# Moving an early sum ahead of the values of the last two key heads, splitting a projection into column groups and moving the denominators in a decode kernel

## Chip, cores, metric

One core of one Trainium2 chip. The metric is the device time of one execution in microseconds; each number given for a kernel is the median of its runs. The kernel before took 190.9 us (three runs, 190.2 to 194.06; the slowest was in a slower state that some executions fall into, over 1.5% above the fastest). TensorE does the matmuls, VectorE and ScalarE the element-wise work. The granted clock is the share of its full speed at which TensorE was allowed to run. The experiments ran in four sessions, each on another chip, so across sessions times are compared by their ratios to the kernel before, which ran beside each.

## The reference

One token for each of two sequences: layer norm, attention over the last 4096 positions of a key and value cache (16 query heads, 8 key heads, head size 256), a dense Mish layer, both added to the input.

```python
xn = _layernorm(x)
q  = (xn @ wq)                       # 2 x 16 heads x 256
k  = k_cache[:, :, Sk - W:, :]       # W = 4096, 8 heads, each for 2 query heads
v  = v_cache[:, :, Sk - W:, :]
p  = softmax(q k^T * 256 ** -0.5)
out = x + (p v).reshape(B, 1, 4096) @ wo + mish(xn @ w1 + b1) @ w2
```

Nearly all of the 77.8 MB that it reads are keys and values, 4 MB of each for every key head.

## The kernel before

The loop goes over the key heads `i`. In turn `i` the keys of head `i` are scored in four pieces (VectorE transposes, TensorE scores, ScalarE exponentials, VectorE transposes p into `pT`), and the values of head `i - 1` are summed. Heads 0 to 5 use `values` (32 matmuls 512 columns wide). Heads 6 and 7 use `values_fixed`: 128 matmuls of only four columns, each with its own weight load of 128 x 128 values. The projection of each head by `wo` adds to one sum, `psE` (2 x 448, `add`). Head 7 alone goes to `psA`, the same sum laid out as four column groups of 112 at partitions 0, 32, 64 and 96 (`add_last`); `carry` copies `psE` into it first.

```python
    def add_last(lhsT, w, start=False, stop=False):
        for n in range(NO):                               # NO = 4 column groups
            nc.tensor.matmul(part(n), lhsT=lhsT, rhs=w[:, n * DO : (n + 1) * DO],
                             start=start, stop=stop, tile_position=(0, n * Q), ...)

    def carry():
        early = consts.tile([Bsz, D], FP32, name="early")
        nc.vector.tensor_copy(out=early[:], in_=psE[:])
        add_last(ident_f[0:Bsz, 0:Bsz], early[:, :], start=True)
    # ... cut ...
    def values_fixed(i):
        state["rec", i] = denominator(i)                  # f32 matmul with ones, reciprocal
        # ... cut: po, vv ...
        for t in range(T):                                # T = 64
            for c in range(ND):                           # ND = 2
                nc.tensor.matmul(po[:, c, :], lhsT=vv[:, t, c, :], rhs=pTv[:, th, 0:Q:HS], ...)
        scale_o(i, po)                                    # oT = po * rec, on VectorE
    # ... cut: loop over i up to Hkv = 8 ...
        else:                                             # i == 8
            mix(i - 2)                                    # head 6: add() into psE
            carry()
        # ... cut ...
        if i == Hkv:
            mix(i - 1)                                    # head 7: add_last() into psA
```

The softmax here doesn't subtract the row's maximum and nothing guards it: scores larger than these inputs give would overflow.

## Time and profile before

| | kernel before |
|---|---|
| time, median of its 3 runs | 190.9 us |
| span in the profile | 189.2 us |
| TensorE instructions of which the trace has records (weight loads and matmuls) | 2154 |
| values of head 6 end | 178.54 us |
| values of head 7 begin | 182.22 us |
| last projection ends | 186.54 us |

The last three rows are read from the chain of what ended last, in order of time, where a line ends at its start plus its length. The prediction below shows that chain.

### The profile page before, as it was taken

How to read it: one execution, taken by the hardware profiler on the slowest of the kernel's cores; microseconds unless marked ns; L12 is line 12 of the kernel's file. 1: busy time of each engine (PE TensorE's matmuls, PEld its weight loads, DVE VectorE, ACT ScalarE, POOL GpSimd, SP SyncE). 2: the span in 40 equal slices, each digit the busy share in tenths (PEclk: the TensorE clock that was granted, in tenths of full speed). 3: DMA queues.
4: the chain of work that ended last, by engine and by line, in shares of the span. 5: the costliest groups of instructions: out<-in, count | busy, mean ns of one | idle time of the engine just before them, and what ended most of it. 6: DMA issues, size and time to landing. Idle time of an engine off the chain costs nothing.

```text
span 189.2 us, 2687 instructions
## 1 busy us (share of the span) xinstructions
PE 152.6 (81%) x1077; PEld 76.2 (40%) x1077; DVE 108.1 (57%) x144; ACT 45.4 (24%) x148; POOL 16.4 (9%) x74
## 2 busy tenths in 40 slices
PE   0396088905989997978995899999996969999983
PEld 0132033901434453425442463436442624464762
DVE  6504497059570995099603983299307986955311
ACT  3004015200242233024222204224312242233201
POOL 7000600300003001200030000300020000000000
PEclk9999669955999999999999657999999999999755
DMA  6999899999999999998999999999999999999970
GB/s 208 429 466 443 380 451 422 430 440 443 416 443 443 436 435 438 436 436 360 489 416 411 436 443 436 440 423 424 456 419 443 419 409 443 430 430 416 414 300 0
DMA packets 4597, 77.82 MB, mean 411 GB/s; under 512 B 485, under 2 KB 1001, under 8 KB 1898
## 3 DMA queue, kind: packets, MB, share of 16 engines
q1 hardware_dynamic: 4580, 77.66, 96.2%
q8 instruction: 8, 0.13, 0.2%
q14 instruction: 3, 0.02, 0.0%
q10 hardware_dynamic: 6, 0.01, 0.0%
HBM read 77.67 MB, written 0.00 MB: 411 GB/s over the span
## 4 chain that ended last, share of the span: by engine, by line
DMA 57%; PE 21%; DVE 19%; ACT 1%; issue 1%; SPq 0%; ACTq 0%; DVEq 0%
DMA k<-in_A_k_cache_dram 57%; DVE kt L414 14%; PE sc L426 8%; PE o L487 4%; PE q L573 4%; PE q L527 3%; DVE pT L452 3%; PE psE L223 2%; PE psA L240 1%; ACT p L440 1%; SPq L112 0%; PE den L468 0%; DVE early L252 0%; DVE osum L548 0%; DVE oTm L556 0%
## 5 line engine op out<-in xcount | busy, mean ns | idle before, releaser
L414 DVE STREAM_TRANSPOSE kt<-k 128x2048 f32<-128x2048 f32 x32 | 73.1, 2288 | 49.4 <-DMA k<-in_A_k_cache_dram 49.4
L426 PE MATMUL sc<-kt,qdiag 128*128 128x512 bf16 x256 | 64.2, 400 | 17.6 <-DVE kt L414 16.9
L440 ACT ACTIVATE p<-sc,off 128x256 bf16<-128x256 f32 x64 | 33.0, 544 | 71.3 <-PE sc L426 70.6
L426 PEld LDWEIGHTS <-qdiag 128*128 128x128 bf16 x256 | 23.8, 99 | 54.1 <-issue 22.5
L487 PE MATMUL o<-v,pT 128*8 128x512 bf16 x192 | 42.5, 379 | 0.0
L487 PEld LDWEIGHTS <-pT 128*8 128x8 bf16 x192 | 17.2, 92 | 22.4
L452 DVE STREAM_TRANSPOSE pT<-p 128x512 bf16<-128x512 bf16 x32 | 21.8, 682 | 6.6 <-ACT p L440 6.5
L292 POOL COPY qdiag<-qt 32x16 bf16<-32x16 bf16 x64 | 12.9, 247 | 121.5 <-PE sc L426 104.7
L496 ACT COPY o_sb<-o 8x512 f32<-8x512 f32 x12 | 6.3, 573 | 36.3 <-PE o L487 36.3
L527 PEld LDWEIGHTS q<-ident_f,o_sb 8*64 8x64 f32 x192 | 13.2, 147 | 3.0 <-issue 3.0
L527 PE MATMUL q<-ident_f,o_sb 8*64 8x4 f32 x192 | 13.7, 203 | 0.0
L440 ACT ACTIVATION_READ_ACCUMULATOR p<-sc,off 128x1 f32 x64 | 11.7, 183 | 0.0
L272 PE MATMUL q_ps<-v,xq 128*128 128x512 bf16 x28 | 8.5, 479 | 3.0 <-DMA v<-in_A_wq_dram 3.0
L223 PE MATMUL psE<-v,act_bf 128*2 128x448 bf16 x14 | 4.2, 471 | 6.6 <-DVE act_bf L360 6.6
L573 PEld LDWEIGHTS <-v 128*128 128x128 bf16 x256 | 7.3, 102 | 0.0
L573 PE MATMUL q<-pT,v 128*128 128x4 bf16 x256 | 7.1, 168 | 0.0
L272 PEld LDWEIGHTS <-xq 128*128 128x128 bf16 x28 | 3.3, 118 | 8.2 <-issue 3.9
L282 DVE CAST q_sb<-q_ps 128x512 bf16<-128x512 f32 x2 | 1.3, 686 | 8.9 <-PE q_ps L272 8.9
L223 PE MATMUL psE<-wo,oTm 128*2 128x448 bf16 x24 | 5.0, 352 | 0.8 <-DVE oTm L556 0.8
L223 PEld LDWEIGHTS <-act_bf 128*2 128x2 bf16 x14 | 1.4, 105 | 9.0 <-DVE act_bf L360 6.7
L282 ACT CAST q_sb<-q_ps 128x512 bf16<-128x512 f32 x2 | 1.1, 589 | 13.5 <-PE q_ps L272 13.5
L193 PE MATMUL xnT_ps<-ident,xn_bf 2*128 2x2 bf16 x7 | 0.5, 166 | 4.6 <-DVE xn_bf L136 4.6
(62 smaller groups left out, 46.6 us busy)
## 6 DMA issues: line engine op xcount, KB each, us to landing
k<-in_A_k_cache_dram SPq DMA_DIRECT2D x7, 4096.0 KB, 29.1
v<-in_A_v_cache_dram SPq DMA_DIRECT2D x7, 4096.0 KB, 27.0
k<-in_A_k_cache_dram SPq DMA_DIRECT2D x2, 2048.0 KB, 26.3
v<-in_B_w_dram SPq DMA_DIRECT2D x2, 1568.0 KB, 24.9
wo<-in_A_wo_dram SPq DMA_DIRECT2D x3, 896.0 KB, 31.0
v<-in_A_wq_dram SPq DMA_DIRECT2D x1, 2048.0 KB, 7.8
v<-in_A_v_cache_dram SPq DMA_DIRECT2D x1, 2048.0 KB, 14.1
v<-in_A_wq_dram SPq DMA_DIRECT2D x1, 1536.0 KB, 11.0
```

Source lines behind the costliest of these rows:

```text
L223: nc.tensor.matmul(psE[:], lhsT=lhsT, rhs=w, start=start, stop=stop, skip_group_check=True)
L272: nc.tensor.matmul(ps[u][:], lhsT=xq[:, s, :, :].rearrange("p j k -> p (j k)"), rhs=wq_sb[:, s, u * N5 : (u + 1) * N5], start=(s == 0), st ...
L282: copy(out=q_sb[:, u * N5 : (u + 1) * N5], in_=ps[u][:])
L292: nc.gpsimd.tensor_copy(out=tv[rows, :, e, j * Q : (j + 1) * Q : HS].rearrange("p n (b h) -> p n b h", b=Bsz), in_=qv[rows, :, h0 : h0 + r ...
L414: nc.vector.transpose(out=kt[:].bitcast(FP32), in_=k[:, half * TH * Dh : (half + 1) * TH * Dh].bitcast(FP32),)
L426: nc.tensor.matmul(psc[:], lhsT=qdiag[i % NW][:, n * NE + e, :], rhs=ktv[:, n, e, :, :], start=(n == 0 and e == 0), stop=(n == NB - 1 and ...
L440: nc.scalar.activation(out=pv[:, b, :, :], in_=sv[:, b, :, :], func=ACT.Exp, scale=scale, bias=off[:, b : b + 1], accum_out=state["rs", i] ...
L452: nc.vector.transpose(out=pT[:], in_=p_t.pop(s)[:])
L487: nc.tensor.matmul(po[:], lhsT=pT_t[i * NH + piece][:, uh * NP * Q : (uh + 1) * NP * Q : HS], rhs=v[:, u * NP : (u + 1) * NP, :].rearrange ...
L496: nc.scalar.copy(out=o_sb[:, u, :, :, :], in_=po[:, u * Dh : (u + 1) * Dh] .rearrange("r (m j) -> r j m", j=NJ) .unsqueeze(2) .to_broadcas ...
L527: nc.tensor.matmul(pqv[:, j, :], lhsT=o_sb[:, u, j, :, :].rearrange("r h m -> r (h m)"), rhs=ident_f[0:NR, u * BR : (u + 1) * BR], start=( ...
L573: nc.tensor.matmul(po[:, c, :], lhsT=vv[:, t, c, :], rhs=pTv[:, th, 0:Q:HS], start=(t == 0 and c == 0), stop=(t == T - 1), skip_group_chec ...
```

## The change

The intent is to take work out of the strict sequence at the end. The copy and entry of the early sum go ahead of head 7's last scores; head 6 is projected straight into the column groups, which cost less time (16 narrow matmuls of head 7 take 0.65 us in the kernel before, 4 full-width ones of head 6 take 1.67, both at a granted clock of 0.50); the denominators are computed in the middle of the values.

```diff
     def values_fixed(i):
-        state["rec", i] = denominator(i)
         ...
         for t in range(T):
+            if t == T // 2:
+                state["rec", i] = denominator(i)
     def mix(kvh):
-        put = add_last if kvh == Hkv - 1 else add
         if kvh < Hkv - NFIX:
             ...  (add() as before, stop at head 5)
         for h in range(rep):
             for c in range(ND):
-                put(...)
+                add_last(...)
     # loop over pieces of head i
                 scores(s)
+                if i == Hkv - 1 and piece == 2:
+                    carry()
     # i == 8
             mix(i - 2)
-            carry()
```

## The prediction

> **What bounds the kernel now.** I read the page first. Its chain that ended last gives 57% of the span to the loads of keys (57% on the line that brings k in), and the DMA row of its 40 slices stands at 8 or 9 from slice 2 to slice 38. For most of the run this is a kernel that moves 77.82 MB at a mean of 411 GB/s. The change touches nothing before the eighth head (i = 7), so what matters is the chain of the last 20 us. I therefore read next the chain in order of time, from its last piece backwards:

> ```profile
> 155.14 1.90 PE sc L426 x8
> 157.03 0.12 PE den L468 x2
> 157.15 7.01 PE o L487 x32
> 164.16 1.85 PE sc L426 x8
> 166.01 1.95 PE q L527 x32
> 167.96 1.85 PE sc L426 x8
> 169.81 1.60 PE psE L223 x8
> 171.41 3.59 PE sc L426 x16
> 175.00 0.12 PE den L468 x2
> 175.12 3.43 PE q L573 x128
> 178.54 0.02 issue
> 178.57 0.18 DVE oT L508
> 178.75 0.04 issue
> 178.79 1.67 PE psE L223 x4
> 180.46 0.02 issue
> 180.48 0.62 DVE early L252
> 181.10 0.04 issue
> 181.15 0.55 PE psA L240 x8
> 181.70 0.52 PE den L468 x2
> 182.22 3.43 PE q L573 x128
> 185.65 0.02 issue
> 185.67 0.18 DVE oT L508
> 185.89 0.65 PE psA L240 x14
> ```

> Columns: start and length in us, engine, tile and line. The reader is to see that from 155 us on no DMA stands in the chain. TensorE works without a break from the last scores to 178.54, and what follows is a strict sequence: values of head 6 (128 matmuls, L573), scaling (L508), its output projection into the full-width sum (L223), the copy of that sum (L252), its entry into the column groups (L240), the denominator of head 7, values of head 7, scaling, projection. Between the two value blocks lie 182.22 - 178.54 = **3.68 us**.

> The second limit is not in the chain, because it is met in time. I looked for it in the timeline of the sync queue and in the table of DMA issues of the last 40 us:

> ```profile
> 164.19 2.73 SPq L379 DMA_DIRECT2D v<-in_A_v_cache_dram  x4
> 171.44 0.81 SPq L408 DMA_DIRECT2D wo<-in_A_wo_dram  x2
> ...
> wo<-in_A_wo_dram SPq DMA_DIRECT2D x2, 224.0 KB, 12.6
> ```

> The last two DMA columns are the size and the us from issue to landing. The values of head 7 are issued in four pieces from 164.19, when the values of head 5 give their buffer back. The same table has the first piece (half the values) 14.1 us after its issue, so at 178.3, and the last two pieces 17.1 us after theirs. With the last issue starting at 166.3 (the view of tile v), they land at about 182.8 and 183.4. The two halves of the output weights of head 7 are issued at 171.44 and 171.8, once head 5 has been projected, and land at about **184.0 and 184.4**. Today the first matmul that needs them starts at 185.89, so they have 1.5 us of slack. A gain larger than that meets them.

> [...] a weight load and matmul of L573, four columns wide, take 3.43 us / 128 = 27 ns, as long in the second block as in the first, though the granted clock is 1.00 from 174 to 176 us and 0.50 from 178 us on (view of windows). These blocks do not depend on the clock, and the change will not shorten them. [...] at the same half clock four full-width matmuls (448 columns, L223) take 1.67 us, and the same four as 16 matmuls of 112 columns in four column groups (L240; the chain shows 14 of them) take 0.65 us. [...]

> **The change, part by part.** The order of instructions of the changed kernel confirms the reading of the diff: the carry stands between the seventh and eighth scores of TensorE's last head, the copy ahead of the last three pT transposes of VectorE, the denominator between the two halves of the values. Nothing else moves; the DMA queue is the same.

> (a) Carry moved ahead. It removes from between the value blocks the copy of 0.62, 0.02 + 0.04 of handing over, and the eight passes of 0.55: -1.23 us. It adds the passes before the last scores. The copy itself should lie beside TensorE's work: the sum is complete at 171.41, VectorE ends its key transpose at 171.56 (169.29 + 2.27 in the timeline), so it runs to about 172.2, while TensorE works on scores until 173.2. The passes cost 0.55 us at most on the path (about half that if the full clock there counts). Net **-0.7 us**, up to -0.95.

> (b) Head 6 in column groups. 4 matmuls of 1.67 us become 16 of 0.65: **-1.0 us**.

> (c) Denominators amid the values. They leave 0.12 us before head 6 and 0.52 before head 7, and come back in the middle of the 128 matmuls. I take the same cost for head 6, and 0.12 to 0.52 for head 7, since the 0.52 stands right behind the carry's f32 passes[...]. The reciprocals were already hidden (rec at 177.20, needed at 178.57; the new one would run near 177.9, needed at 179.1). Worth **0 to -0.4 us**.

> Sum on TensorE: -1.7 to -2.35 us. As a clock: scores end at 175.3 to 175.55; values of head 6 end at 178.8 to 179.1; the projection starts 0.25 later, ends at 179.7 to 180.0; values of head 7 (3.43 + denominator) end at 183.3 to 183.95. On the way the pieces of v are due at about 180.0 (landed 178.3), 183.3 (landed 182.8) and 183.5 (landed 183.4): no wait, or one of a tenth or two. Scaling (0.24) brings the projection to 183.5 to 184.2. There it meets the output weights at 184.0 and 184.4. With half of its 0.65 us left behind the second landing it ends at about 184.75, where it ended at 186.54. So of a possible 2.35 us **about 1.8 us** arrive, and the DMA cuts the rest. 190.9 - 1.8 = **189.1 us**, a ratio of 0.991.

> **The rivals.**

> Rival 1: the DMA becomes the bound entirely. The sync queue's order and the release of its buffers (164.19, 171.44) are before the moved work, so the last landing stays near 184.4. For it: the DMA engines are busy at 0.88 still from 182 to 183 us and at 0.45 in the next. If in other executions they end half a microsecond or a microsecond later against TensorE, the gain is 0.8 to 1.3 us: 189.6 to 190.1. It cannot eat the whole gain unless it lands past 186, which the trace does not support.

> Rival 2: the carry in mid-loop is a new wait. [...]if the copy waits behind VectorE's queue, the last scores wait too, then the exponentials and pT of head 7. Against it: the copy is due at 172.2 and needed at 173.2, a slack of 1 us, and sums of head 7, needed amid its values at about 181.7, were ready at 177.2. If the order were worse than it seems and the copy came behind the pT transpose that waits for ACT until 174.41, the loss would be some 1.8 us and the whole change worth nothing: 190.9. The instruction order speaks against that.

> Rival 3: the full gain and more. If the loads end earlier than I put them, [...]TensorE's 2.35 us arrive: 188.5. A gain above 2% would need 3.8 us, more than everything between the value blocks (3.68). Nothing in the change offers that.

> **Range and chances.** The three times before lie 3.9 us apart (190.2, 190.9, 194.06), wider than the whole effect, so the spread of runs sets the range more than the mechanism does. From Rival 3 less some luck to Rival 1 plus some ill luck: 187.9 to 190.4. The effect of 0.9% is well inside 2% either way. Faster by over 2% would need a slow draw of the kernel before: 0.03. Slower: 0.01. Within 2%: 0.96.

> **What the profile of the changed kernel would show.** (a) holds if the copy of early starts near 171.6 and L240 runs at about 173.2 without idle time named after the copy; (b) if the first projection is 16 matmuls in about 0.65 us instead of 4 in 1.67; (c) if the block of values of head 7 with its denominator is 3.55 to 3.95 us long. The gap between the last matmul of one value block and the first of the next should fall from 3.68 to about 0.9 us. The cut by DMA is right if a wait for wo, or for the last piece of v, stands before the last L240 or in the last L573, a few tenths long; its absence with a gain of 2.2 us or more would make Rival 3 right. The prediction is wrong if the gain is under 0.8 us with the gap closed, which means a DMA wait longer than I worked out, or if TensorE sits idle before L240 at 173 us.

0.7 to 0.95 us for (a), 1.0 for (b) and 0 to 0.4 for (c) make the 1.7 to 2.35 us on TensorE, of which about 1.8 were expected to arrive, 190.9 - 1.8 = 189.1 us. The "about half" in (a) is an estimate from the kernel before: the granted clock was 1.00 from 172 to 174 us, where the passes go, and 0.50 from 181 to 182, where they were, and a full-width matmul of L223 took 1.60 / 8 = 0.20 us at 1.00 and 1.67 / 4 = 0.42 at 0.50. That a late copy would hold up the last scores too, as Rival 2 has it, is supposition and was not tested. Why the denominator took 0.52 us before head 7 and 0.12 before head 6 was not shown.

## More of the kernel before

The table of DMA queues (columns: packets, MB, share of the time of the 16 engines):

```profile
q1 hardware_dynamic: 4580, 77.66, 96.2%
q8 instruction: 8, 0.13, 0.2%
```

The second line is a queue that no line of the kernel issues. Its eight packets have 16,384 bytes each, 0.13 MB in all.

## The result, and the profile after

The changed kernel took **190.47 us** (six runs, 190.35 to 190.92), the kernel before 191.18 in the same sessions (six runs). The ratio of the fast runs is 0.9981, with a 95% interval of 0.9957 to 1.0004: the same within 2%. Ratios are the mean time of one kernel's fast runs over that of the other's of the same rounds, so not quite the ratio of the medians. The predicted 189.1 us was missed, and 190.47 lies just above the range's end of 190.4.

This is the end of the chain of what ended last, of the changed kernel:

```profile
173.36 0.30 PE psA L240 x8
173.66 1.84 PE sc L426 x8
175.50 1.69 PE q L574 x64
177.19 0.22 PE den L468 x2
177.41 1.72 PE q L574 x64
...
179.37 0.47 PE psA L240 x16
179.84 1.14 PE q L574 x38
180.98 1.16 issue
182.13 0.86 PE q L574 x26
182.99 0.42 PE den L468 x2
183.42 1.77 PE q L574 x64
...
185.44 0.65 PE psA L240 x10
```

What the prediction wanted between the two value blocks happened: the carry costs 0.30 us at 173.36, the projection of head 6 takes 0.47 instead of 1.67, and head 7's values begin at 179.84 instead of 182.22, 2.38 us earlier. But after 38 of those 128 matmuls stands a line that nobody expected: 1.16 us of "issue", time in which TensorE waited for nothing that the profile shows. After it the denominator and the rest follow, and the last projection ends at 186.09. Of the 2.38 us only 0.45 are left.

The idle is not a wait of the program. In the instruction order, head 7's first 64 value matmuls need the first half of v and pT; the wait for the next piece of v stands at matmul 65, and the new pT at matmul 33. No wait stands at number 39. The timeline has 39 weight loads and 38 matmuls before the idle: it parts a matmul from its own weight load.

### The profile page after: what moved, and what is told of

Read it like the earlier page. It is cut to its first block, busy times and chain, and to the rows that moved or that the text cites. A ratio compares the mean times of both kernels' runs of the same rounds, so it can differ in the third digit from the quotient of the medians.

```text
span 188.7 us, 2710 instructions
## 1 busy us (share of the span) xinstructions
PE 151.0 (80%) x1089; PEld 74.9 (40%) x1089; DVE 108.9 (58%) x144; ACT 45.4 (24%) x148; POOL 16.3 (9%) x74
## 2 busy tenths in 40 slices
DMA packets 4597, 77.82 MB, mean 412 GB/s; under 512 B 485, under 2 KB 1001, under 8 KB 1898
## 4 chain that ended last, share of the span: by engine, by line
DMA 57%; DVE 21%; PE 17%; issue 1%; ACT 1%; SPq 0%; ACTq 0%; DVEq 0%
DMA k<-in_A_k_cache_dram 57%; DVE kt L414 17%; PE sc L426 7%; PE q L574 4%; PE o L487 4%; DVE pT L452 3%; PE q L527 1%; PE psE L223 1%; PE psA L240 1%; ACT p L440 1%; SPq L112 0%; PE den L468 0%; DVE sums L461 0%; DVE osum L548 0%; DVE oTm L556 0%
## 5 line engine op out<-in xcount | busy, mean ns | idle before, releaser
L426 PE MATMUL sc<-kt,qdiag 128*128 128x512 bf16 x256 | 64.8, 403 | 17.2 <-DVE kt L414 17.2
L426 PEld LDWEIGHTS <-qdiag 128*128 128x128 bf16 x256 | 24.0, 100 | 54.2 <-issue 22.4
L487 PE MATMUL o<-v,pT 128*8 128x512 bf16 x192 | 42.5, 379 | 0.0
L487 PEld LDWEIGHTS <-pT 128*8 128x8 bf16 x192 | 17.2, 92 | 22.4
L527 PEld LDWEIGHTS q<-ident_f,o_sb 8*64 8x64 f32 x192 | 11.6, 133 | 2.8 <-issue 2.8
L527 PE MATMUL q<-ident_f,o_sb 8*64 8x4 f32 x192 | 12.1, 195 | 0.0
L223 PE MATMUL psE<-v,act_bf 128*2 128x448 bf16 x14 | 5.2, 566 | 6.6 <-DVE act_bf L360 6.6
L272 PE MATMUL q_ps<-v,xq 128*128 128x512 bf16 x28 | 7.9, 452 | 2.1 <-DVE xq L263 2.1
L574 PE MATMUL q<-pT,v 128*128 128x4 bf16 x256 | 7.7, 169 | 1.2 <-issue 1.2
L223 PE MATMUL psE<-wo,oTm 128*2 128x448 bf16 x24 | 5.0, 352 | 1.7 <-DVE oTm L556 1.7
L223 PEld LDWEIGHTS <-act_bf 128*2 128x2 bf16 x14 | 1.6, 121 | 9.6 <-DVE act_bf L360 6.7
## 6 DMA issues: line engine op xcount, KB each, us to landing
v<-in_A_v_cache_dram SPq DMA_DIRECT2D x1, 2048.0 KB, 14.1
```

The source lines that it names most:

```text
L223: nc.tensor.matmul(psE[:], lhsT=lhsT, rhs=w, start=start, stop=stop, skip_group_check=True)
L272: nc.tensor.matmul(ps[u][:], lhsT=xq[:, s, :, :].rearrange("p j k -> p (j k)"), rhs=wq_sb[:, s, u * N5 : (u + 1) * N5], start=(s == 0), st ...
L426: nc.tensor.matmul(psc[:], lhsT=qdiag[i % NW][:, n * NE + e, :], rhs=ktv[:, n, e, :, :], start=(n == 0 and e == 0), stop=(n == NB - 1 and ...
L487: nc.tensor.matmul(po[:], lhsT=pT_t[i * NH + piece][:, uh * NP * Q : (uh + 1) * NP * Q : HS], rhs=v[:, u * NP : (u + 1) * NP, :].rearrange ...
L527: nc.tensor.matmul(pqv[:, j, :], lhsT=o_sb[:, u, j, :, :].rearrange("r h m -> r (h m)"), rhs=ident_f[0:NR, u * BR : (u + 1) * BR], start=( ...
```

## The experiments

To compare profiles I use the length of the end, from the start of head 5's values (L487 x32 in the chain, 157.15 us in the kernel before) to the end of the last projection. It is 29.39 us before (29.38 in a second profile, experiment 7) and 28.83 after; it leaves out what happens earlier. "Record" means a weight load or matmul of TensorE in the trace, counted from the start of the execution.

**1. Shift the count of instructions.** Small transposes with unused result, near 17 us, where TensorE waits.

```diff
     project()
+    pad = ps_m.tile([P, NS, Bsz], BF16, tag="m", name="pad")
+    for u in range(24):       # second run: 64
+        nc.tensor.transpose(pad[:, u % NS, :], xn_bf[:, u % NS, :, :]..., ident[0:Bsz, 0:Bsz])
```

> The changed kernel with 24 small transposes (48 TensorE instructions, result unused) added near 17 us, where TensorE waits. Theory F (TensorE's instructions come in blocks of 256 by 16 KB packets, and in the changed kernel the last fast stretch runs out of them): the 1.16 us of idle inside the values of head 7, now after the 38th of 128 matmuls, moves with the count of instructions to after about the 14th; its length stays at 1.0 to 1.6 us and the time within 0.3 us of the changed kernel. Theory W (the idle is a wait for something in that place: a piece of v, the output weights, a pT, the throttle): it stays after the 38th matmul or at the same time, 180.98 to 182.13 us.

> The same with 64 small transposes (128 instructions). Theory F: the boundary of the block moves 128 instructions forward, to the last five or so matmuls of head 6's values, where the fetch, asked for at the last scores, comes nearly in time (idle 0 to 0.4 us); the next boundary, which lay behind the end, now falls into the second half of head 7's values, after about 36 of its 64 matmuls (100 of 128), with an idle of 0.5 to 1.4 us. Time within 0.6 us of the changed kernel. Theory W: the idle stays after the 38th matmul of head 7, 1.16 us.

Times: 190.51 and 190.59 us (ratios to the kernel before 0.9989, interval 0.9957 to 1.002, and 0.9990, interval 0.9952 to 1.0028). The chain with 24 transposes:

```profile
179.85 0.46 PE q L574 x14
180.31 1.39 issue
181.69 1.48 PE q L574 x50
```

And with 64:

```profile
182.29 0.96 PE q L574 x36
183.25 1.33 issue
184.59 0.91 PE q L574 x28
```

The idle is after the 14th matmul in the one and after the 36th of the second half in the other, exactly where the count put it, and at other times. In the changed kernel, with 24 transposes and with 64, it stands after record 1963, 1963 and 2219, and 2219 is 1963 + 256. No wait for data or clock keeps step with unused transposes 160 us earlier. W is out. At the earlier boundary of the run with 64, at the end of head 6's values, there was no idle, as expected at the low end: its packet ended at 176.90 and the block was needed at 178.85.

**2. Part the fast stretch.** The same instructions, but the first half of head 6's values stands ahead of the last scores (16 slow records, 1.84 us).

```diff
                 if s == NSTEP - 1:
+                    values_fixed(i - 1, 0)     # t < T // 2 of head 6
                 scores(s)
     ...
-                values_fixed(i - 1)
+                values_fixed(i - 1, 1 if i < Hkv else None)
```

> The changed kernel with the first half of head 6's values (64 matmuls) put ahead of the last scores, so that slow scores part the fast stretch. The same instructions in another order. Theory F: between the boundaries of the blocks, about 1707 and 1963 in the count of TensorE's records, now lie the last scores of 1.84 us, the block lasts about 5.5 us instead of 3.9, the fetch of about 5.4 us is hidden, and the idle of 1.16 us shrinks to 0 to 0.2: the last projection ends near 184.9 instead of 186.09, the time is 1.0 to 1.3 us shorter than that of the changed kernel, about 189.3. The output weights (landed at about 184.2 to 184.4) are then just met. Theory W: same idle, same time, 190.5.

Time 189.54 us, ratio to the kernel before 0.9936 (interval 0.9908 to 0.9964), where the changed kernel had 0.9981. The end lasts 27.75 us. The chain of its last 5 us, without any issue line:

```profile
180.01 1.80 PE q L577 x64
181.81 0.42 PE den L468 x2
182.23 1.72 PE q L577 x64
```

The packet came at 177.97 to 178.91 and the block was needed at 180.97. F holds, and the gain over the changed kernel, 0.9936 against 0.9981 or 0.9 us, is a little less than expected. A part was lost to a new wait of my own making: the projection of head 6 waited 0.76 us for oT, as VectorE had the last pT transpose and head 7's sums ahead of it.

**3. Take the load away.** A quarter of head 7's values is loaded and used four times, in the changed kernel and in the kernel before. Their outputs are wrong, which doesn't matter for the times. (The comparison with the reference passed nevertheless, so it does not see a change of this size. It says nothing about correctness.)

```diff
-            load_v(i, ... (0, T // 2, 13 * T // 16, 15 * T // 16, T))
+            load_v(i, ... (0, T // 4))
-                    lhsT=vv[:, t, c, :],
+                    lhsT=vv[:, t if i < Hkv - 1 else t % (T // 4), c, :],
```

> Wrong result on purpose: of head 7's values only the first quarter is loaded (1 MB instead of 4) and used four times; all TensorE instructions and their order are as in the changed kernel. The DMA engines fall idle near 175 us. Theory F: the fetch asked for at about 176.7 no longer queues behind the load of v; its packet starts about 1.2 us later instead of 3.1, ends at about 178.9, and TensorE has the block at about 180.2, before it needs it at 180.7: no idle, end of the last projection about 184.7, 1.2 to 1.5 us shorter than the changed kernel. If the idle stays though no data wait is left, F holds only with a latency that does not depend on the load; if it goes, W with a data wait is not excluded by this run alone.

> Wrong result on purpose: the kernel before with the same cut as the thin kernel (a quarter of head 7's values loaded, used four times). It measures what TensorE's part of the change is worth by itself, with no load and no late fetch in the way. Theory F: the kernel before had no wait for instructions or data in its end, so nothing changes, last projection ends at 186.3 to 186.6 (186.54 with the full load); against the thin changed kernel (184.50) this is 1.8 to 2.1 us, within the prediction's sum of 1.7 to 2.35. If it ends much earlier, the end of the kernel before was bound by the DMA after all and the prediction's sum was wrong.

The changed kernel took 189.04 us (ratio 0.9912, interval 0.9882 to 0.9942) and ended at 184.50, with no idle: the packet started 0.33 us after TensorE had passed the boundary of the block instead of 3.03 (about 1.2 had been expected). Its chain from the start of head 7's values:

```profile
179.67 1.79 PE q L574 x64
181.46 0.42 PE den L468 x2
181.88 1.72 PE q L574 x64
```

The kernel before took 190.87 (ratio 0.9996, interval 0.9974 to 1.0019) and ended at 186.71, 0.1 later than expected. Their ends last 27.32 and 29.39 us. So TensorE's part of the change by itself is worth 2.07 us of the end in the profile, within the prediction's sum of 1.7 to 2.35; by the ratios it is 1.6 us, just below it. With the load, the changed kernel's end is 28.83 - 27.32 = 1.51 us longer: the idle of 1.16, 0.21 in the first 64 value matmuls (2.00 us without the idle, against 1.79), 0.10 in the projection of head 6 (0.47 against 0.37) and 0.05 in the last 64.

**4. Undo the third part.** The denominators stand ahead of the values again.

```diff
     def values_fixed(i):
+        state["rec", i] = denominator(i)
     ...
-            if t == T // 2:
-                state["rec", i] = denominator(i)
```

> The changed kernel with its third part undone: the denominators stand again ahead of the values. Theory F: the idle for the fetch ends at the same time, about 182.1, but the denominator of head 7 (0.42 us) is done before it, inside the time that is waited anyway, instead of after it. So 92 matmuls remain after the idle and no denominator: the last projection ends at about 185.5 instead of 186.09, the time is 0.4 to 0.6 us below that of the changed kernel, about 190.0; the idle itself is shorter, 0.8 to 1.0 us. Without F (the denominators cost the same in both places, as the prediction had it): same time to 0.2 us either way.

Time 190.11 us, ratio 0.9960 (interval 0.9947 to 0.9974). Its end lasts 28.50 us, 0.33 less than the changed kernel's; the times agree (190.11 against 190.47, 0.36 less). Both are just short of the 0.4 to 0.6 expected. The run beside it and the run of the changed kernel are of different sessions, and the 0.33 us is one profile of each, so the difference of their ratios, 0.2%, is a sign and not more. The chain shows why:

```profile
181.62 0.94 issue
182.56 2.61 PE q L573 x92
```

The idle is shorter, 0.94 us, because the denominator of head 7 (0.52 us) fills part of the time that is waited anyway. In the change it comes after the idle and costs its full 0.42 us. This idle too stands after record 1963.

**5. Smaller data packets.** Head 7's values in eight equal pieces, 4 KB for each partition. (In the changed kernel the four pieces travel in packets of 16,384, 10,240, 4,096 and 2,048 bytes, by the packet records.)

```diff
-  (0, T // 2, 13 * T // 16, 15 * T // 16, T)
+  (0, *range(T // 8, T + 1, T // 8))
```

> The changed kernel with the values of head 7 loaded in eight equal pieces (4 KB for each partition) instead of four (16, 10, 4 and 2 KB). It asks whether the fetch waits behind the size of the data packets. If the fetch packet queues behind a few large packets: it starts at 177.9 to 179.2 instead of 179.86 and the idle shrinks to 0 to 0.6 us, time 190.0 or less. If it waits behind the whole queue, or for a reason that has nothing to do with packet size, it starts near 179.9 again, the idle stays at 1.0 to 1.4 us, and the time at 190.4.

Time 190.50 us, ratio 0.9971 (interval 0.9956 to 0.9987). The profile fell in a slow execution, so only its fetch is read: TensorE passed the boundary at 179.54, the packet started at 182.38, 2.84 us later, and an idle of 1.09 us stood after record 1963 again. Smaller packets did not bring the fetch forward. That it waits for the loads is shown by experiment 3 (0.33 us from the boundary to the packet with little load, 3.03 with the load); behind what exactly it queues stays open. TensorE went on 1.56 us after the packet's end, 5.28 after the boundary.

The fetches of these runs (without experiment 5) side by side, from the packet records and the records of TensorE. The boundary passed is the one 256 records before that of the idle; "reached" is the start of the last record before the next boundary, and TensorE goes on with the next record.

| run | boundary passed | packet | next boundary reached | goes on |
|---|---|---|---|---|
| before | 176.63 | 179.71 to 180.65 | 183.33 | at once |
| changed | 176.83 | 179.86 to 180.80 | 180.81 | 182.13 |
| 24 transposes | 176.30 | 179.31 to 180.27 | 180.14 | 181.69 |
| 64 transposes | 178.85 | 182.21 to 183.13 | 183.09 | 184.59 |
| interleaved | 175.16 | 177.97 to 178.91 | 180.94 | at once |
| denominators in front | 177.22 | 180.26 to 181.19 | 181.45 | 182.56 |
| changed, little load | 176.76 | 177.09 to 178.25 | 180.60 | at once |

In the four runs of the table with an idle, TensorE goes on 1.33 to 1.46 us after the end of the packet, and 5.3 to 5.7 us after the boundary. The kernel before spent 6.7 us between the same two boundaries, because its slow sequence of projection, copy and carry lay between them. So, as an estimate from these numbers, it had 1.0 to 1.4 us to give before the fetch bound it, and no shortening of that stretch alone could gain more.

In all five runs with an idle (with experiment 5), the packets started 2.8 to 3.4 us after the boundary, took 0.88 to 0.96 us, and TensorE went on 1.3 to 1.6 us after their end. In two places without an idle the delay to the packet's start was shorter under load, 2.1 and 2.2 us (the control of experiment 7 and the earlier boundary of the run with 64 transposes), and with little load it was 0.3 to 0.5 us.

**6. Is the DMA bound of the prediction behind it?** The interleaved kernel, with the last pT transpose and the sums of head 7 put behind the scaling of head 6 on VectorE, run twice; and the same with little load.

```diff
-                if s == NSTEP - 1:
-                    turn_p(s)
     ...
                 values_fixed(i - 1, 1 if i < Hkv else None)
+                if i < Hkv:
+                    turn_p(NSTEP - 1)
```

> The interleaved kernel (first half of head 6's values ahead of the last scores) with one more move: the last pT transpose and the sums of head 7 are put behind the scaling of head 6 on VectorE. In the interleaved run the projection of head 6 waited 0.76 us for oT, because the scaling stood behind them (sums ended at 179.23, values of head 6 at 178.8). Theory F and this reading: the wait falls to about 0.26, values of head 7 begin near 179.5 instead of 180.0, the fetch is still hidden (block ready near 180.2, needed at 180.4 or later), and now the DMA bound of the prediction is met: output weights and last piece of v land at 183.3 to 184.3, so the last projection ends at 184.4 to 184.7 instead of 184.85; gain over the interleaved kernel 0.2 to 0.45 us, time about 189.2. If the fetch is late after all, an idle of some tenths stands inside head 7's values and nothing is gained.

> The same kernel as the deferred one; its profile had fallen in an execution of 191.57 us in which TensorE's end came 2.7 us later than in the others while the loads came at the usual time, so it did not test the meeting of the two. A profile of one of the usual executions (189.4 to 189.8) is wanted. Expected as before: projection of head 6 waits 0.26, and either a wait before head 7's last matmuls or projection (the DMA bound: last v and output weights seen at 183.3 to 184.3) with an end at 184.6 to 184.9, or no wait and an end at 184.4. The times of 189.42 to 189.78, equal to the interleaved kernel's, speak for the first.

> Wrong result on purpose: the deferred kernel with a quarter of head 7's values loaded. If the load of v and wo bounds the deferred kernel, this one is faster than it by 0.2 to 0.6 us (about 189.0, last projection at 184.2 to 184.4, like the thin changed kernel's 184.50). If it is no faster, TensorE is the bound of the deferred kernel and the DMA bound of the prediction is not met at all.

The first session gave 189.50 us (ratio 0.9925, interval 0.9912 to 0.9939), no better than the interleaved kernel's 189.54. Its profile fell in an execution of 191.57 us. There the granted clock was 0.50 from 148 to 156 us, TensorE came late by 2.9 us (head 5's values start at 160.00, in the interleaved kernel at 157.10), and no wait for a load stands in its end. It tests nothing of the meeting. The second session gave 189.77 (ratio 0.9971, interval 0.9919 to 1.0022; one of its four runs took 191.63). Its profile, of an execution of 189.91, has what the prediction had looked for. In the chain:

```profile
171.80 13.13 DMA wo<-in_A_wo_dram
...
184.97 0.46 PE psA L240 x8
```

and among the waits of TensorE from 170 to 189 us (columns: us in all, times, longest):

```profile
PE q L577 <- DMA v<-in_A_v_cache_dram: 0.5, 1, 0.5
```

The last half of the output weights releases the second half of the last projection at 184.97, and the second piece of v had made the values wait 0.5 us, before matmul 65. The end came at 185.43, later than the 184.6 to 184.9 expected: in this execution the last packets of the output weights ended at 184.59, in the interleaved one at 184.01. With little load the same kernel takes 188.93 us (ratio 0.9901) and its end lasts 27.24 us instead of 28.31. So behind the fetch stands the DMA bound, seen in one execution; it is the likely reason why the deferral gained nothing over the interleaving. The fetch had nothing to spare there either: the packet ended at 179.17 and TensorE crossed into the block at 180.50, 1.33 us later, the least delay that any run with an idle shows.

**7. Controls.** The interleaving and deferral on the kernel before; and the kernel before itself once more.

> The kernel before with only the interleaving and the deferral (first half of head 6's values ahead of the last scores; last pT and sums of head 7 behind the scaling of head 6). Control for theory F: the kernel before has no late fetch, so parting its fast stretch gains nothing: last projection at 186.3 to 186.7 as in the kernel before (186.54), time the same to 0.3 us. If it gains about 1 us here too, the interleaving helps for a reason of its own and the interleaved run does not show the fetch.

> The kernel before once more, unchanged. Its fast executions fall into two groups, spans of 188.4 to 188.9 and of 189.0 to 189.3 us, and the control with the interleaved kernel before ended 0.7 us early because its projection of head 6 (L223 x4) ran at the full clock, 0.93 us instead of 1.67. Theory C (the clock granted near 179 us makes the two groups): a profile of an execution of about 188.5 shows L223 x4 at 0.93 us and the passes of the carry at 0.3 to 0.4; one of about 189.2 shows 1.67 and 0.55 again. An execution of 188.5 with L223 at 1.67, or of 189.2 with 0.93, is against C.

The control took 190.06 us, ratio 0.9971 (interval 0.9946 to 0.9997), and its end 28.46 us instead of 29.39. My expectation of no gain was wrong. The chain of the control has the cause in one line:

```profile
179.04 0.93 PE psE L223 x4
```

The projection of head 6 took 0.93 us instead of 1.67, because the granted clock was still 1.00 from 178 to 180 us, where the kernel before has 0.50; the passes of the carry took 0.37 instead of 0.55. Together 0.92 us, all of the 0.93 gained. So the interleaving has an effect of its own, and in the one profile of each it goes through the clock. By its time alone the interleaved run would therefore not show the fetch; its chain does, with experiments 1 and 3. There the clock gave little: the projection of head 6 took 0.37 us instead of 0.47. The missing idle is 1.16, the first 64 values of head 7 are 0.20 faster, the last 64 0.05, and 0.43 was lost before the projection: 1.08 in all, the difference of the two ends.

The kernel before again took 190.92 us (ratio to itself 0.9981, which shows what such a ratio is worth here). Its profile, with a span of 189.1, has L223 x4 at 1.67 us, as theory C wanted. The spans of its fast executions reach from 188.4 to 189.5, most of them near 188.5 or 189.2, and the clock may be what parts these; no execution near 188.5 was profiled, so this stays open.

## Why the prediction was wrong, point by point

- **(a), carry ahead: right.** Copy from 171.69, passes at 173.29 to 173.66 with no wait for the copy, 0.30 us on the path, the lower of the two costs given. Rival 2 did not happen. (The prediction puts the carry "between the seventh and eighth scores" of the last head. That head is scored in four pieces, and the carry stands between the third and the fourth; the sums do not depend on it.)
- **(b), column groups: right.** 1.67 us became 0.47, against 0.65 expected, as the clock was still full for part of it (0.87 on average from 178 to 180 us, 0.50 in the kernel before). That part was luck: the prediction had reckoned with the half clock. What halves it was not tested: in the kernel before it was 0.80 from 176 to 178 us, then 0.50, although TensorE's busy time by the profile was 2.00 us in those 2 us and in the 2 us before.
- **(c), denominators amid the values: wrong in sign.** Worth 0 to -0.4 by the prediction; undoing it shortened the end by 0.33 us (one profile of each). With little load it is worth nothing: the two denominators take 0.22 + 0.42 us, in the kernel before 0.12 + 0.52. With the load, the one of head 7 moved from before an idle to after it.
- **The sum on TensorE: right where nothing interferes.** 1.7 to 2.35 predicted, 2.07 measured with little load. Of it, 0.28 us is the clock: the projection of head 6 took 0.37 us there, at the full clock, and not 0.65.
- **The step that failed** is the one that turned this sum into a clock: "values of head 7 (3.43 + denominator) end at 183.3 to 183.95. On the way the pieces of v are due [...]: no wait, or one of a tenth or two." They ended at 185.19. They began at 179.84, within the range worked out for that, and took 5.35 us instead of 3.55 to 3.95; 1.16 of it is the idle, which did not stand in the sum. The list of pieces also left out the second one, for which the table of issues has no landing: the wait of 0.5 us in the deferred kernel was for it. I had checked that stretch against waits of the program and landings of data, and not against the supply of instructions. The wait that took the place of the removed work was the fetch of TensorE's next 256 instructions, with a packet that started 3.03 us after the boundary under load and 0.33 without.
- **Rival 1, the DMA as the bound: right in kind, hidden.** No wait for v or wo stands in the changed kernel. It came once the fetch was out of the way, in the deferred kernel. The prediction's own sign of being wrong did come, a gain under 0.8 us with the gap closed (0.71 us instead of 3.68), but what it was said to mean, a longer DMA wait, did not.
- **The size.** 1.8 us predicted; 0.56 in the end of the profile, 0.36 by the ratio (0.0019 of 190.9), 0.71 by the medians, in which two slow runs of the kernel before (194.06 and 193.8) count. The ratio, 0.9981, is the one that the kernel before gave against itself in experiment 7, so the times do not show a gain of the changed kernel at all; the chain shows one.
- **The chances were right:** within 2%, safe since all that lay between the value blocks is less than that. The range was too tight on its upper side, as its rivals lacked this one.

The best version found keeps the change and interleaves: 189.54 us, 0.9936 of the kernel before.

## What to carry to other kernels

Before shortening a stretch of many small TensorE instructions, count them: find the 16 KB packets of the instruction queue in the trace, see how long they take from boundary to use under the load of that moment (5.3 us or more here), and compare with the time in which 256 of the shortened stretch would run (some 3.5 us here). Where the stretch is too fast, put slow work (long matmuls) among the fast instead of shortening it further, as experiment 2 did: with 1.84 us of scores between, the idle of 1.16 us was gone. An "issue" line amid equal instructions, at a place that no wait of the program marks, is tested by adding a few unused instructions far ahead of it: if it moves by their count, as here from the 38th matmul to the 14th with 24 transposes, the fetch is the likely cause.
